# A fused attention and mixture-of-experts kernel: one product step and its loads in other places, and the start of the program issued in other pieces

## The chip, the cores and the metric

The kernel runs on one core of one Trainium2 chip. The metric is the device time of one execution in microseconds (us). The kernel before takes 1173.28 us, the median of three runs that lie between 1173.11 and 1174.34 us.

## The reference

Four batches of N = 5056 tokens have channels C = 256. Attention is taken over channels, so the score matrix of a batch is only 256 x 256, and its result goes token by token to one of eight experts.

```python
# attention over channels, one batch of four: q, k, v are (5056, 256)
qn = q / (norm(q, axis=tokens) + 1e-6)
kn = k / (norm(k, axis=tokens) + 1e-6)
s  = kn.T @ qn / tau                    # (256, 256)
a  = softmax(s, axis=-1)
x  = v @ a                              # (5056, 256)
# experts: x of all batches is (20224, 256), E = 8, F = 1024
logits = x @ w_gate + modality_bias[modality_id]
e = argmax(logits); gate = softmax(logits)[e]
out[token] = gate * (relu(x[token] @ w1[e]) @ w2[e])
```

## The kernel before

**Steps.** A batch is cut into NS = 10 steps of 512 tokens (128 partitions x 4; the last is shorter). `kq_pieces(b, s)` handles step s of batch b: `load` brings q and k (512 KB each) by SP's queue; `split` makes a high and a low half of each on ACT (L320) and DVE (L321), unless the step stands in `WHOLE`, in which case the products are taken from the loaded tile as it is; `mm` adds k'q to the 256 x 256 sum `g` on PE (L365); `square` takes squares on ACT (L344) and adds them on DVE (L346) for the norms. Steps 0 to 5 of batch 1 are whole; its steps 6 to 9 are split. Loaded tiles of batch 1 take turns in two buffers from step 4 on, so step 6 is loaded into the buffer that step 4 had and waits for step 4's squares.

**Routing steps.** After the ten steps and the softmax of batch 0, the program runs through routing steps g = 0 to 39 (10 to a batch). Routing step g takes 512 rows of v, either transposed on PE (L565) or, from g = 6 on, by a transposing DMA into `T` (L534) and four copies `pl` (L511); forms x = v a on PE (`xp`, L585); adds the bias of the modality (L598); counts and places the rows; and scatters them by GpSimd (`xs`, L474) to the region of their expert in DRAM. PLAN says which steps of batch 1 are multiplied in which routing step: here step 5 at g = 6, steps 6 and 7 at g = 8, steps 8 and 9 at g = 9.

**Slots.** From g = 6 on (`first_block`), blocks of 512 rows of one expert, called slots, run beside the routing steps: slot 0 at g = 6, slot 1 at g = 7, and so on. A slot fetches its rows by a transposing DMA (`Tx`, L766) and their gates (`gt`, L769), loads w1 and w2 in two halves each (`w1r`, `w2r`, 512 KB each, L788 and L792), splits them on ACT (L811) and DVE (L818), and runs eight first products `hp_0` to `hp_7` (L845), whose relu goes to `hh` on ACT (L848) and `hl` on DVE (L849), and eight second ones (`y`, L866). Slot 0's rows are of g = 0 to 2. HELD keeps back the scatters of g = 3 and g = 4: they are sent in the following routing step once its rows of tile 3 are copied.

**Order.** The program is written as lists of pieces that `_interleave` mixes by their shares, and each engine then runs its instructions strictly in the order of its own list. SP issues almost all loads; a load whose buffer is still in use or whose source isn't written holds up all that stands behind it. The small loads (`itau`, `wg_sb`, `mb_sb`, the modalities `modraw`) are on SP's queue among the loads of batch 0.

```python
PLAN = [[], [2], [], [3], [4], [], [5], [], [6, 7], [8, 9]]
HELD = {3: 3, 4: 3}
...
if g - 1 in HELD:
    t = HELD[g - 1]
    own.insert(t + 1, lambda: va[g - 1][4]([copied[g, t]]))
```

Of the kernel before, what the change touches and what calls it, by code (L numbers as in the profile page):

```python
# [35 lines left out]
def kernel(  # L36
# [14 lines left out]
    P = 128  # L51
# [28 lines left out]
    PLAN = [[], [2], [], [3], [4], [], [5], [], [6, 7], [8, 9]]  # L80
# [6 lines left out]
    HELD = {3: 3, 4: 3}  # L87
# [87 lines left out]
    turning = []  # L175
    written = [[] for _ in range(G)]
# [14 lines left out]
    def load_small():  # L191
        itau = small["itau"] = const.tile([P, 1], F32, name="itau")
        nc.sync.dma_start(itau, tau.partition_broadcast(P))
        nc.vector.reciprocal(itau, itau)
        wg_sb = small["wg"] = const.tile([P, CH, E], F32, name="wg_sb")
        nc.sync.dma_start(wg_sb, wg.rearrange("(h p) e -> p h e", p=P))
        mb_sb = small["mb"] = const.tile([P, 2, E], F32, name="mb_sb")
        nc.sync.dma_start(
            mb_sb.rearrange("p m e -> p (m e)"), mb.rearrange("m e -> (m e)").partition_broadcast(P)
        )  # L200
# [8 lines left out]
    def load_mod():  # L209

        full = B * (NS - 1)
        raw = p2.tile([P, TT * D], F32, tag="yo", name="modraw").bitcast(I32)
        nc.vector.memset(raw[full // 32 * 32 : R, 2 * PL * TT : 2 * STEP], 0)
        m32 = mod.bitcast(I32).rearrange("(b n) -> b n", b=B)
        for b in range(B):
            nc.sync.dma_start(
                raw[b * (NS - 1) : (b + 1) * (NS - 1), 0 : 2 * STEP],
                m32[b, 0 : 2 * (NS - 1) * STEP].rearrange("(s w) -> s w", w=2 * STEP),
            )
        nc.sync.dma_start(raw[full:R, 0 : 2 * PL * TT], m32[:, 2 * (NS - 1) * STEP : 2 * N])  # L220
        turn["raw"] = raw
# [46 lines left out]
    filled = []  # L268
    acc = {}

    def kq_pieces(b, s, behind=(), later=None):
# [18 lines left out]
        def load():  # L290
            if b == 0:
                begin()
            for n, src, tag in (("q", q, "w1r"), ("k", k, "w2r")):
# [5 lines left out]
                if b == 0 and s == 0:  # L299
                    st[n + "rows"] = rows  # L300
                else:
                    nc.sync.dma_start(st[n][:pp], rows)
            if b == 0 and s == 0:
                for h in range(2):
                    ts = slice(2 * h, 2 * h + 2)
# [23 lines left out]
        def square(h):  # L329
            ts = slice(2 * h, 2 * h + 2)  # L330
            a = acc[b]
            for n, o in (("q", 0), ("k", C)):
# [11 lines left out]
                act(nc.scalar.activation(sq[:pp], st[n][:pp, ts, :], AF.Square))  # L344
                if not first:
                    dve(nc.vector.tensor_tensor(a[:pp, :, o : o + C], a[:pp, :, o : o + C], sq[:pp], ALU.add))  # L346
# [400 lines left out]
    def block_pieces(g, slot, picked, tail):  # L747
# [13 lines left out]
        def load_x():  # L761
# [3 lines left out]
            for ins in (  # L765
# [13 lines left out]
                if slot == 1:  # L779
                    turning.append(ins.ins)  # L780
# [148 lines left out]

    for s in range(NS):  # L930
# [46 lines left out]
    def product(n):  # L977
        g, b, i = tasks[n]
        if n not in products:
            products[n] = list(kq_pieces(  # L980
                b, i, (lambda: routed.get(g, routed[g - 1])) if b == 1 else (),
                squares.setdefault(g + (3 if g + 2 == first_block else 1), [])
# [11 lines left out]
    def products_of(g):  # L994

        out = []
        for n, (at, b, i) in enumerate(tasks):
            if at == g:
                out += [lambda n=n: ask(n)] if g <= first_block else []
                out += product(n)[1:]  # L1000
                if g >= first_block and (b, i) != (1, NS - 1):
                    out.append(lambda n=n: ask(n + (1 if g == first_block else 2)))
        if g == first_block + 1:
            out.append(lambda: ask(min(n for n in range(len(tasks)) if tasks[n][0] > g) + 1))
# [12 lines left out]
    for g in range(G):  # L1017
# [15 lines left out]
        if g - 1 in HELD:  # L1033
            t = HELD[g - 1]
            own.insert(t + 1, lambda: va[g - 1][4]([copied[g, t]]))
        turn = []
# [20 lines left out]
        _interleave(*streams)  # L1057
        if waiting and waiting[0][0] <= g + 1 - lag(g + 1):
            blk = waiting[0][1]
            once(blk, "load")  # L1060
            if blk["slot"] == 0:
                turned(blk["evicted"][-1])
# [94 lines left out]
```

## Time and profile before

| | |
|---|---|
| median of three runs | 1173.28 us |
| profiled execution | 1176.94 us |
| its span, from the first to the last instruction | 1175.1 us |
| mean granted clock of TensorE | 0.998 |
| PE busy | 1152.9 us (98%) |
| DVE busy | 919.4 us (78%) |
| ACT busy | 806.5 us (69%) |

The page gives, for the slowest core, the busy time of each engine, the busy share in slices, the chain that ended last, and the costliest groups of instructions. Times inside the span are counted from its start. A row of the timeline has the start, the duration, the engine, the line of the kernel and the tile that is written and read, and in brackets the idle time just ahead of it with what ended it.

### The profile page before, as it was taken

To read this page: it belongs to the slowest core of one execution; us is meant where nothing else is said; L and a number is where in the kernel's file an instruction comes from. 1 tells how busy PE (TensorE), PEld (TensorE's weight loads), DVE (VectorE), ACT (ScalarE), POOL (GpSimd) and SP (SyncE) were. 2 spreads that over 40 slices of the span, in tenths; PEclk is the share of its full clock that TensorE was granted. 3 is DMA by queue.
4 is the path that set the end of the run, shared out by engine and by line. 5 is a ranking of instruction groups with operands and counts; after the bars stand their busy time and mean duration, and the time that the engine had idled before them with its cause. 6 is when DMAs were issued, how large, how long until landed. Compare 5 with 4: busy or idle time off the path is not lost.

```text
span 1175.1 us, 23436 instructions
## 1 busy us (share of the span) xinstructions
PE 1152.9 (98%) x7748; PEld 1054.9 (90%) x7748; DVE 919.4 (78%) x2590; ACT 806.5 (69%) x1655; POOL 386.9 (33%) x345
## 2 busy tenths in 40 slices
PE   8997999999999999999999999999999999999997
PEld 7886889999999999999999999999999999999997
DVE  6787889898788888888888888878767776685552
ACT  6676877877777777687776777767666666555552
POOL 0054334323333333333333333333333333344122
PEclk9999999999999999999999999999999999999999
DMA  8969999689777677758777766665875665565420
GB/s 311 295 223 235 274 234 261 175 238 218 199 202 198 196 197 207 202 166 228 211 204 209 207 197 165 169 175 162 218 202 174 190 173 156 143 170 144 127 91 30
DMA packets 285843, 228.38 MB, mean 194 GB/s; under 512 B 185064, under 2 KB 243944, under 8 KB 285712
## 3 DMA queue, kind: packets, MB, share of 16 engines
q1 hardware_dynamic: 270032, 185.19, 60.0%
q0 software_dynamic: 15680, 41.61, 10.3%
q8 instruction: 62, 1.02, 0.4%
q14 instruction: 69, 0.57, 0.2%
HBM read 128.79 MB, written 43.43 MB: 147 GB/s over the span
## 4 chain that ended last, share of the span: by engine, by line
PE 84%; issue 7%; DVE 3%; DMA 2%; POOL 2%; ACT 1%; SPq 0%; POOLq 0%; ACTq 0%; DVEq 0%
PE y L866 32%; PE hp L845 32%; PE g L365 10%; PE xp L585 9%; POOL out_dram L474 2%; DMA pl<-T 1%; DMA Tx<-xs 1%; DVE hl L849 0%; DMA xs<-x,pi 0%; DVE inv L398 0%; PE vtp L567 0%; PE gw L434 0%; DVE w2l L818 0%; SPq L511 0%; DMA k<-in_k_dram 0%
## 5 line engine op out<-in xcount | busy, mean ns | idle before, releaser
L866 PE MATMUL y<-w2h,hh 128*128 128x256 f32 x1256 | 354.5, 282 | 0.0
L866 PE MATMUL y<-w2l,hh 128*128 128x256 f32 x1256 | 351.2, 280 | 0.0
L866 PE MATMUL y<-w2h,hl 128*128 128x256 f32 x1256 | 349.5, 278 | 0.1
L474 POOL DMA_INDIRECT xs<-x,pi x160 | 199.1, 1245 | 362.8 <-DVE pr L708 182.8
L474 POOL DMA_INDIRECT out_dram<-yo,gt x158 | 175.2, 1109 | 391.6 <-ACT hh L848 296.8
L845 PE MATMUL hp<-xh,w1h 128*128 128x512 f32 (+1 forms) x640 | 250.0, 391 | 6.1 <-ACT xh L830 3.5
L845 PE MATMUL hp<-xl,w1h 128*128 128x512 f32 (+1 forms) x640 | 250.1, 391 | 0.0
L845 PE MATMUL hp<-xh,w1l 128*128 128x512 f32 (+1 forms) x640 | 248.8, 389 | 0.0
L866 PEld LDWEIGHTS y<-w2h,hh 128*128 128x128 f32 x1256 | 236.4, 188 | 9.5 <-issue 0.2
L866 PEld LDWEIGHTS y<-w2l,hh 128*128 128x128 f32 x1256 | 236.4, 188 | 8.4
L849 DVE SCALAR_TENSOR_TENSOR hl<-hp,hh 128x512 fp32r<-128x512 f32 (+1 forms) x320 | 217.0, 678 | 34.3 <-ACT hh L848 30.8
L866 PEld LDWEIGHTS y<-w2h,hl 128*128 128x128 f32 x1256 | 235.3, 187 | 0.4 <-DVE hl L849 0.3
L848 ACT ACTIVATE hh<-hp 128x512 fp32r<-128x512 f32 (+1 forms) x320 | 188.7, 590 | 59.9 <-PE hp L845 58.7
L811 ACT CAST w1h<-w1r 128x512 fp32r<-128x512 f32 x160 | 99.3, 621 | 169.5 <-PE hp L845 141.2
L818 DVE TENSOR_TENSOR w1l<-w1r,w1h 128x512 fp32r<-128x512 f32 x160 | 110.0, 687 | 90.6 <-ACT w1h L811 87.3
L845 PEld LDWEIGHTS hp<-xh,w1l 128*128 128x128 f32 x640 | 120.1, 188 | 25.8
L845 PEld LDWEIGHTS hp<-xh,w1h 128*128 128x128 f32 x640 | 119.9, 188 | 20.3 <-ACT xh L830 3.7
L845 PEld LDWEIGHTS hp<-xl,w1h 128*128 128x128 f32 x640 | 120.2, 188 | 13.7 <-DVE xl L831 0.4
L818 DVE TENSOR_TENSOR w2l<-w2r,w2h 128x512 fp32r<-128x512 f32 x160 | 109.9, 687 | 12.0 <-ACT w2h L811 9.3
L811 ACT CAST w2h<-w2r 128x512 fp32r<-128x512 f32 x160 | 100.3, 627 | 20.3 <-PE y L866 18.4
L597 DVE COPY x<-xp 128x256 uint16<-128x256 uint16 x136 | 57.1, 420 | 52.3 <-ACT x L596 50.7
L585 PE MATMUL xp<-ah,vh 128*128 128x264 f32 x320 | 92.6, 291 | 1.2 <-DVE L L598 1.2
(162 smaller groups left out, 1827.6 us busy)
## 6 DMA issues: line engine op xcount, KB each, us to landing
w1r<-in_moe_w_dram SPq DMA_DIRECT2D x80, 512.0 KB
w2r<-in_moe_w_dram SPq DMA_DIRECT2D x80, 512.0 KB
q<-in_q_dram SPq DMA_DIRECT2D x35, 512.0 KB
k<-in_k_dram SPq DMA_DIRECT2D x35, 512.0 KB
pl<-T SPq DMA_DIRECT2D x120, 128.0 KB
v<-in_v_dram SPq DMA_DIRECT2D x6, 512.0 KB
xs<-x,pi POOLq DMA_INDIRECT x160
out_dram<-yo,gt POOLq DMA_INDIRECT x158
```

The lines of the kernel that those rows point to most:

```text
L365: nc.tensor.matmul(gram[b][:, m, :], x, y, start=first and m == 0 and i == 0, stop=last and i == len(seq) - 1, skip_group_check=True,)
L474: ins = nc.gpsimd.indirect_dma_start(out=dst, out_offset=bass.IndirectOffsetOnAxis(ap=idx, axis=0), in_=rows, in_offset=None, bounds_check ...
L585: nc.tensor.matmul(xp[:, 0:DE], a[:, h, t * P : (t + 1) * P], w[:, h, :], start=i == 0, stop=i == len(seq) - 1,)
L597: copied[g, t] = nc.vector.tensor_copy(planes[:, 0, :], halfwords[:, 0, :]).ins
L811: ins = nc.scalar.copy(hi, src).ins
L818: evicted[-1] = [ins, nc.vector.tensor_tensor(lo, src, hi.bitcast(F32), ALU.subtract).ins]
L845: nc.tensor.matmul(hp[:, 0:rows], w[:, h, fs], x[:, h, 0:rows], start=i == 0, stop=i == len(seq) - 1)
L848: relu = nc.scalar.activation(hh[:, 0:rows], hp[:, 0:rows], AF.Relu).ins
L849: low = nc.vector.scalar_tensor_tensor(hl[:, 0:rows], hp[:, 0:rows], 0.0, hh[:, 0:rows].bitcast(F32), ALU.max, ALU.subtract).ins
L866: ins = nc.tensor.matmul(y, a[:, tsl], w[:, j % 2, :], start=(j == 0 and i == 0 and t % per == 0), stop=(j == NJ - 1 and i == 2), skip_gro ...
```

## The change

Six things are edited.

1. Twenty products of ones (128 x 128, bf16, nobody reads them) stand ahead of everything else on PE.
2. The q and k of batch 0's step 0 are loaded in three pieces (a quarter, a quarter and a half) instead of two, those of step 1 in two instead of one.
3. The small loads and the modalities are issued by GpSimd instead of SP.
4. PLAN puts step 5 of batch 1 at g = 5, step 6 at g = 7, step 7 at g = 8, and 8 and 9 at g = 9. `products_of` asks for the loads of a routing step ahead of its products; those of step 5 are asked for at g = 4.
5. The scatters of g = 3 no longer wait for copies of g = 4: they are sent first in g = 5, and wait for slot 0's `Tx` and `gt`.
6. The squares of step 3 are taken at the end of g = 5, behind slot 0's first weight splits and ahead of its rows; those of steps 4 and 5 at the end of g = 6. Before, step 5's stood in line with its products.

```diff
-    PLAN = [[], [2], [], [3], [4], [], [5], [], [6, 7], [8, 9]]
+    PLAN = [[], [2], [], [3], [4], [5], [], [6], [7], [8, 9]]
-    HELD = {3: 3, 4: 3}
+    HELD = {3: None, 4: 3}
...
-        nc.sync.dma_start(itau, tau.partition_broadcast(P))
+        nc.gpsimd.dma_start(itau, tau.partition_broadcast(P))
...
-            if b == 0 and s == 0:
-                for h in range(2):
-                    ts = slice(2 * h, 2 * h + 2)
+            if b == 0 and s < 2:
+                for ts in (slice(0, 1), slice(1, 2), slice(2, 4)) if s == 0 else (slice(0, 2), slice(2, 4)):
                     for n in ("q", "k"):
                         nc.sync.dma_start(st[n][:, ts, :], st[n + "rows"][:, ts, :])
...
-                if slot == 1:
-                    turning.append(ins.ins)
+                if slot < 2:
+                    (rows_in, turning)[slot].append(ins.ins)
...
+    warm = ps2.tile([P, 512], F32, tag="aux", bufs=3, name="warm")
+    for i in range(20):
+        nc.tensor.matmul(warm[:, 0:P], onesb, onesb, start=True, stop=True, skip_group_check=True)
+
     for s in range(NS):
         run(kq_pieces(0, s))
...
-                squares.setdefault(g + (3 if g + 2 == first_block else 1), [])
+                squares.setdefault({3: 6, 4: 7, 5: 7}.get(g, g + 1), [])
...
-        for n, (at, b, i) in enumerate(tasks):
-            if at == g:
-                out += [lambda n=n: ask(n)] if g <= first_block else []
-                out += product(n)[1:]
-                if g >= first_block and (b, i) != (1, NS - 1):
-                    out.append(lambda n=n: ask(n + (1 if g == first_block else 2)))
-        if g == first_block + 1:
-            out.append(lambda: ask(min(n for n in range(len(tasks)) if tasks[n][0] > g) + 1))
+        mine = [n for n, task in enumerate(tasks) if task[0] == g]
+        if g <= first_block + 1:
+            out += [lambda n=n: ask(n) for n in mine]
+        if g + 2 == first_block:
+            out += [lambda n=n: ask(n + 1) for n in mine]
+        for n in mine:
+            out += product(n)[1:]
+            if g == first_block + 1:
+                out.append(lambda n=n: ask(n + 1))
+            if g > first_block and tasks[n][1:] != (1, NS - 1):
+                out.append(lambda n=n: ask(n + 2))
...
-        if g - 1 in HELD:
+        if HELD.get(g - 1) is not None:
             t = HELD[g - 1]
             own.insert(t + 1, lambda: va[g - 1][4]([copied[g, t]]))
+        if g + 1 == first_block:
+            own.insert(0, lambda: va[g - 2][4](rows_in))
...
+        if g + 1 == first_block:
+            gap += list(zip(("act", "dve"), waiting[0][1]["evicted"][-1]))
+            run(squares.pop(first_block))
...
             if blk["slot"] == 0:
-                turned(blk["evicted"][-1])
+                turned(newest)
```

**SP's queue, from the transposing load of routing step 8 on, before.** `T_1565` and `T_1611` are the v of routing steps 8 and 9, `q_6` and `k_6` are step 6 of batch 1, the w1r and w2r here are slot 2's weights, and `Tx_1726` is slot 2's rows. What the dots leave out are register instructions.

```order
L534 DMA_TRANSPOSE T_1565<-in_v_dram 128x4x512
L302 DMA q_6_1621<-in_q_dram 128x1024
L302 DMA k_6_1623<-in_k_dram 128x1024
L511 DMA pl_1594<-T_1565 64x2x512 x4
...
L788 DMA w1r_0_1709<-in_moe_w_dram 128x2x512
...
L792 DMA w2r_0_1710<-in_moe_w_dram 128x4x256
L534 DMA_TRANSPOSE T_1611<-in_v_dram 128x4x448
...
L788 DMA w1r_1_1713<-in_moe_w_dram 128x2x512
...
L792 DMA w2r_1_1714<-in_moe_w_dram 128x4x256
...
L766 DMA_TRANSPOSE Tx_1726<-xs 128x4x512
...
L769 DMA gt_1727<-xs 128x4x2
L302 DMA q_7_1888<-in_q_dram 128x1024
```

**The same stretch now.** The numbers behind the names are others: `T_1582` and `T_1624` are the same two loads, `Tx_1747` is slot 2's rows.

```order
L539 DMA_TRANSPOSE T_1582<-in_v_dram 128x4x512
...
L793 DMA w1r_0_1730<-in_moe_w_dram 128x2x512
L516 DMA pl_1607<-T_1582 64x2x512 x4
...
L797 DMA w2r_0_1731<-in_moe_w_dram 128x4x256
...
L793 DMA w1r_1_1734<-in_moe_w_dram 128x2x512
L539 DMA_TRANSPOSE T_1624<-in_v_dram 128x4x448
...
L797 DMA w2r_1_1735<-in_moe_w_dram 128x4x256
...
L771 DMA_TRANSPOSE Tx_1747<-xs 128x4x512
...
L774 DMA gt_1748<-xs 128x4x2
L305 DMA q_6_1784<-in_q_dram 128x1024
L305 DMA k_6_1786<-in_k_dram 128x1024
L305 DMA q_7_2073<-in_q_dram 128x1024
```

`q_6` and `k_6` stood second and third behind the load of routing step 8. They now stand behind the load of routing step 9, slot 2's weights and slot 2's rows; w1r's first half stands ahead of `pl`.

**ACT, slot 1's second and third relu and what stands around them, before.** `hh_2` and `hh_3` are of slot 1, `yo` is slot 0's output, `x_1401` is routing step 7's, `vh_1799` routing step 8's.

```order
L596 COPY x_1401<-xp_1_1786 128x256
L811 CAST w2h_3_1884<-w2r_1_1331 128x512
L571 CAST vh_1799<-vt_0_1803 128x512
L596 COPY x_1401<-xp_2_1818 128x256
L848 ACTIVATE hh_2_1835<-hp_2_1828 128x512
L596 COPY x_1401<-xp_3_1856 128x256
L659 COPY x_1401<-tokid 128x4
L320 CAST qs_6_0_2156<-q_6_1621 128x2x256
L320 CAST ks_6_0_2157<-k_6_1623 128x2x256
L848 ACTIVATE hh_3_1873<-hp_3_1866 128x512
```

**The same place now.** `sq_6_0` are squares of step 6; the other names are those of before with other numbers.

```order
L816 CAST w2h_3_1933<-w2r_1_1368 128x512
L601 COPY x_1434<-xp_2_1855 128x256
L322 CAST qs_6_0_1823<-q_6_1784 128x2x256
L346 ACTIVATE sq_6_0_q<-q_6_1784 128x512
L853 ACTIVATE hh_2_1884<-hp_2_1877 128x512
L322 CAST qs_6_1_1937<-q_6_1784 128x2x256
L322 CAST ks_6_0_1824<-k_6_1786 128x2x256
L346 ACTIVATE sq_6_0_k<-k_6_1786 128x512
L523 COPY vt_0_1840<-pl_1607 128x512
L601 COPY x_1434<-xp_3_1905 128x256
L322 CAST ks_6_1_1938<-k_6_1786 128x2x256
L853 ACTIVATE hh_3_1922<-hp_3_1915 128x512
```

The high halves of q of step 6 (`qs_6_0`) stood behind `hh_2`; they now stand ahead of it, with a square between the two, and those of k stand ahead of `hh_3`.

**PE, the beginning of slot 1's fourth first product, before.** In these names the first number behind `hp`, `xh` and `w1h` is the slot and the second the product.

```order
L845 MATMUL hp_1_3_1866<-xh_1_1553,w1h_1_1_1613 128x512
L845 MATMUL hp_1_3_1866<-xl_1_1554,w1h_1_1_1613 128x512
L845 MATMUL hp_1_3_1866<-xh_1_1553,w1l_1_1_1614 128x512
L845 MATMUL hp_1_3_1866<-xh_1_1553,w1h_1_1_1613 128x512
L845 MATMUL hp_1_3_1866<-xl_1_1554,w1h_1_1_1613 128x512
L845 MATMUL hp_1_3_1866<-xh_1_1553,w1l_1_1_1614 128x512
L866 MATMUL y0_1_1842<-w2h_1_0_1487,hh_1_1_1770 128x256
```

**The same place now.**

```order
L590 MATMUL xp_7_3_1905<-ah_0_463,vl_7_1433 128x264
L850 MATMUL hp_1_3_1915<-xh_1_1570,w1h_1_1_1626 128x512
L850 MATMUL hp_1_3_1915<-xl_1_1571,w1h_1_1_1626 128x512
L370 MATMUL g_1_510<-qs_1_6_0_1823,ks_1_6_0_1824 128x256 x2
L850 MATMUL hp_1_3_1915<-xh_1_1570,w1l_1_1_1627 128x512
L850 MATMUL hp_1_3_1915<-xh_1_1570,w1h_1_1_1626 128x512
L850 MATMUL hp_1_3_1915<-xl_1_1571,w1h_1_1_1626 128x512
L850 MATMUL hp_1_3_1915<-xh_1_1570,w1l_1_1_1627 128x512
L370 MATMUL g_1_510<-qs_1_6_0_1823,ks_1_6_0_1824 128x256 x10
L871 MATMUL y0_1_1891<-w2h_1_0_1510,hh_1_1_1795 128x256
```

The first twelve products of step 6 (`g_1`, from `qs_1_6_0` and `ks_1_6_0`) now stand inside `hp_1_3`, behind its first two matmuls. Before, they stood within slot 2.

## Rows read from the trace of the kernel before

**Rows 1.** From the page: the busy time of each engine, and the chain that ended last by engine.

```profile
PE 1152.9 (98%) x7748; PEld 1054.9 (90%) x7748; DVE 919.4 (78%) x2590; ACT 806.5 (69%) x1655; POOL 386.9 (33%) x345
...
PE 84%; issue 7%; DVE 3%; DMA 2%; POOL 2%; ACT 1%; SPq 0%; POOLq 0%; ACTq 0%; DVEq 0%
```

**Rows 2.** What PE waited for between 80 and 160 us: engine, tile and line that waits, what ended the wait, us in total, times, longest.

```profile
PE hp L845 <- ACT xh L830: 3.5, 1, 3.5
PE hp L845 <- DVE hl L849: 2.6, 3, 1.7
PE g L365 <- DVE qs L321: 1.6, 2, 1.1
PE xp L585 <- DVE L L598: 1.2, 1, 1.2
PE g L365 <- DVE ks L321: 0.2, 1, 0.2
```

**Rows 3.** Stretches of the span as PE saw them: the stretch and its length, busy time of PE with its matmuls, the granted clock, the share of the DMA engines, GB/s.

```profile
0.00:5.00 5.00, 0.37 (x1) 1.00 0.55 172
5.00:10.00 5.00, 5.00 (x13) 1.00 0.95 358
10.00:15.00 5.00, 5.00 (x25) 1.00 1.03 419
...
94.00:97.00 3.00, 0.11 (x1) 1.00 0.96 286
97.00:100.00 3.00, 3.00 (x15) 1.00 1.36 235
...
150.00:160.00 10.00, 8.02 (x55) 1.00 1.11 191
...
170.00:500.00 330.00, 329.99 (x2280) 1.00 0.77 208
...
1168.00:1172.00 4.00, 0.00 (x0) 0.78 0.26 81
```

**Rows 4.** Timeline of PE, its first row.

```profile
4.63 13.55 PE L365 MATMUL g<-q,k 128*128 128x256 f32 x50 [4.63 <-DMA k<-in_k_dram]
```

**Rows 5.** Timeline of SP's queue from 84 to 145 us. The duration of a row is the time for which the issue held up the queue.

```profile
88.14 2.46 SPq L766 DMA_TRANSPOSE Tx<-xs  x1
...
92.53 6.09 SPq L534 DMA_TRANSPOSE T<-in_v_dram  x1
...
106.80 3.30 SPq L766 DMA_TRANSPOSE Tx<-xs  x1
...
110.98 0.39 SPq L788 DMA_DIRECT2D w1r<-in_moe_w_dram  x1
...
112.11 6.78 SPq L534 DMA_TRANSPOSE T<-in_v_dram  x1
118.99 0.52 SPq L302 DMA_DIRECT2D q<-in_q_dram  x1
119.57 0.42 SPq L302 DMA_DIRECT2D k<-in_k_dram  x1
...
124.34 0.41 SPq L788 DMA_DIRECT2D w1r<-in_moe_w_dram  x1
...
126.60 2.34 SPq L534 DMA_TRANSPOSE T<-in_v_dram  x1
...
131.54 6.27 SPq L766 DMA_TRANSPOSE Tx<-xs  x1
...
138.49 0.49 SPq L302 DMA_DIRECT2D q<-in_q_dram  x1
```

**Rows 6.** Timeline of ACT, the rows that waited for a DMA or stand at step 6.

```profile
94.50 1.38 ACT L518 COPY xt<-Tx 128x512 uint16<-128x512 uint16 x2 [3.93 <-DMA Tx<-xs]
...
116.25 0.62 ACT L811 CAST w1h<-w1r 128x512 fp32r<-128x512 f32 x1 [2.19 <-DMA w1r<-in_moe_w_dram]
...
126.61 1.42 ACT L518 COPY vt<-pl 128x512 uint16<-128x512 uint16 x2 [0.50 <-DMA pl<-T]
128.31 0.62 ACT L811 CAST w1h<-w1r 128x512 fp32r<-128x512 f32 x1 [0.27 <-DMA w1r<-in_moe_w_dram]
...
133.88 0.62 ACT L320 CAST qs<-q 128x512 fp32r<-128x512 f32 x1
```

**Rows 7.** Timeline of PE: slot 1's fourth first product, and the products of step 6.

```profile
133.32 0.39 PE L845 MATMUL hp<-xh,w1h 128*128 128x512 f32 x1
133.55 0.40 PE L845 MATMUL hp<-xl,w1h 128*128 128x512 f32 x1
133.79 0.39 PE L845 MATMUL hp<-xh,w1l 128*128 128x512 f32 x1
...
154.90 0.28 PE L365 MATMUL g<-qs,ks 128*128 128x256 f32 x1
156.25 0.38 PE L365 MATMUL g<-qs,ks 128*128 128x256 f32 x1 [1.08 <-DVE qs L321]
156.85 1.45 PE L365 MATMUL g<-qs,ks 128*128 128x256 f32 x10 [0.22 <-DVE ks L321]
...
159.66 0.38 PE L365 MATMUL g<-qs,ks 128*128 128x256 f32 x1 [0.52 <-DVE qs L321]
```

More of the change, by code (lines that the diff above doesn't have):

```diff
@@ L175 @@
     turning = []
+    rows_in = []
     written = [[] for _ in range(G)]
@@ L192, in load_small @@
         itau = small["itau"] = const.tile([P, 1], F32, name="itau")
-        nc.sync.dma_start(itau, tau.partition_broadcast(P))
+        nc.gpsimd.dma_start(itau, tau.partition_broadcast(P))
         nc.vector.reciprocal(itau, itau)
         wg_sb = small["wg"] = const.tile([P, CH, E], F32, name="wg_sb")
-        nc.sync.dma_start(wg_sb, wg.rearrange("(h p) e -> p h e", p=P))
+        nc.gpsimd.dma_start(wg_sb, wg.rearrange("(h p) e -> p h e", p=P))
         mb_sb = small["mb"] = const.tile([P, 2, E], F32, name="mb_sb")
-        nc.sync.dma_start(
+        nc.gpsimd.dma_start(
             mb_sb.rearrange("p m e -> p (m e)"), mb.rearrange("m e -> (m e)").partition_broadcast(P)
@@ L215, in load_mod @@
         for b in range(B):
-            nc.sync.dma_start(
+            nc.gpsimd.dma_start(
                 raw[b * (NS - 1) : (b + 1) * (NS - 1), 0 : 2 * STEP],
@@ L219, in load_mod @@
             )
-        nc.sync.dma_start(raw[full:R, 0 : 2 * PL * TT], m32[:, 2 * (NS - 1) * STEP : 2 * N])
+        nc.gpsimd.dma_start(raw[full:R, 0 : 2 * PL * TT], m32[:, 2 * (NS - 1) * STEP : 2 * N])
         turn["raw"] = raw
@@ L268 @@
     filled = []
+    newest = []
+    gap = []
     acc = {}
@@ L302, in load @@
                     nc.sync.dma_start(st[n][:pp], rows)
-            if b == 0 and s == 0:
-                for h in range(2):
-                    ts = slice(2 * h, 2 * h + 2)
+            if b == 0 and s < 2:
+                for ts in (slice(0, 1), slice(1, 2), slice(2, 4)) if s == 0 else (slice(0, 2), slice(2, 4)):
                     for n in ("q", "k"):
@@ L343, in square @@
                         sq = p3.tile([P, 2, C], F32, tag="vt", name=f"sq_{b}_{s}_{h}_{n}")
-                act(nc.scalar.activation(sq[:pp], st[n][:pp, ts, :], AF.Square))
+                squared = nc.scalar.activation(sq[:pp], st[n][:pp, ts, :], AF.Square)
+                act(squared)
                 if not first:
-                    dve(nc.vector.tensor_tensor(a[:pp, :, o : o + C], a[:pp, :, o : o + C], sq[:pp], ALU.add))
+                    added = nc.vector.tensor_tensor(a[:pp, :, o : o + C], a[:pp, :, o : o + C], sq[:pp], ALU.add)
+                    dve(added)
+                    newest[:] = [squared.ins, added.ins]
         def mm(h):
@@ L980, in product @@
             products[n] = list(kq_pieces(
-                b, i, (lambda: routed.get(g, routed[g - 1])) if b == 1 else (),
-                squares.setdefault(g + (3 if g + 2 == first_block else 1), [])
+                b, i, (lambda: gap if g + 3 == first_block else routed.get(g, routed[g - 1])) if b == 1 else (),
+                squares.setdefault({3: 6, 4: 7, 5: 7}.get(g, g + 1), [])
                 if b == 1 and (g < first_block or i == NS - 1) else None,
```

## Prediction

> **What bounds the kernel now.** I read the page's busy times and chain first, then what PE waited for, then PE's stretches, and last the queues of SP, ACT and PE around the places that the diff moves. PE is busy for 98% of the span and holds 84% of the chain [rows 1]: PE's matmuls set the time, and only what PE loses can be won. The stretches show where it loses [rows 3]: the first 5 us hold one matmul, the next 5 us 13 where the 5 us after that hold 25, so the first dozen run at half rate (1.2 and then 2.4 GHz); some us go between 80 and 160, among them 2.9 us between 94 and 97 and 2.0 us between 150 and 160; from 170 to 500 us PE loses 0.01 of 330 us. So whatever PE has gained or lost by 170 us is carried to the end, since from there the order of its work is that of before. The waits between 80 and 160 us add up to some 9 us [rows 2]: 3.5 for slot 0's rows (`xh`), 2.6 for `hl`, 1.8 for the halves of steps 6 and 7 (`qs`, `ks`), 1.2 for the biased logits `L`.
>
> **The start.** PE's first product waits 4.63 us for k [rows 4]. The pieces of a quarter bring this forward, and the twenty products of ones let the clock rise while PE waits. The half rate costs (25 - 13) x 0.2 = 2.4 us. But the loads bound this: three steps are 3.15 MB, and the first 10 us move 0.86 + 1.79 = 2.65 MB; at 419 GB/s the third step's last byte comes at 11.2 us at the earliest [rows 3]. Before, the first two steps (32 matmuls in the trace, two to a product) end at 10 + (32 - 14) x 0.2 = 13.6 us, so at most 13.6 - 11.2 = 2.4 us are gained by then, and at least nothing; I take 1.0, nearer to the low end since the DMA engines are already at a share of 0.95 and the same bytes go through them. The small loads by GpSimd share those engines; I cost them at nothing, covered by the loads of steps 5 to 9, which come well ahead of PE. If that cover failed, PE would wait within the first 43 us and the 1.0 would go.
>
> **Around slot 0.** The squares of step 3 leave ACT and DVE ahead of the logits on which PE waits 1.2 us, and the scatters of g = 3 leave GpSimd while `Tx` is on its way: `Tx` is issued at 88.14 and its first reader starts at 94.50, 6.4 us later [rows 5, 6], where PE waits 3.5 us. The square of step 5 leaves the stretch in which `hl` is late. Bounds are 0 and 3.5 + 1.2 + 2.6 = 7.3 us, of which the weight splits and `pl`, which stay, hold the most; I take 1.7, the longest wait for `hl`, about a quarter.
>
> **Step 6 of batch 1, the term that decides.** Before, its loads are issued at 118.99 and 119.57, right behind the load of routing step 8 [rows 5]; ACT has its first half at 133.88 [rows 6], and PE multiplies it only from 154.90 on [rows 7], so some 30 us lie between issue and use. The change takes this slack from both sides. The loads now stand behind the load of routing step 9, all of slot 2's weights and slot 2's `Tx` and `gt`; the use comes ahead of `hh_2` on ACT and behind two matmuls of slot 1's `hp_3` on PE, which is where PE stands at 133.79 [rows 7].
>
> When are they issued? Three times a transposing load is followed within some 5 us by a second one, and the second holds up SP's queue: the end of its issue lies 92.53 + 6.09 - 88.14 = 10.5, 112.11 + 6.78 - 106.80 = 12.1 and 131.54 + 6.27 - 126.60 = 11.2 us behind the issue of the first, where one that has no other just ahead takes 2.34 to 3.30 [rows 5]. The load of routing step 9 can't go before `pl` has emptied its tile: it was issued at 126.60, when the last `pl` landed (its reader starts at 126.61) [rows 5, 6]. With the 1 MB of step 6 no longer ahead, and slot 0 a little earlier, I put it between 124.6 and 126.6 and take 125.2. Then slot 2's `Tx` has left the queue at 125.2 + 11.2 = 136.4; `gt` and q go by 136.9, k 0.6 later at 137.5, as before [rows 5]. A load of 512 KB takes 128.31 - 124.34 = 4.0 to 116.25 - 110.98 = 5.3 us from issue to its reader here [rows 5, 6]; I take 4.7, so k is there at 142.2, and with one copy of 0.62 by ACT [rows 6] the first product can run at 142.8. The ends are 124.6 + 10.5 + 0.5 + 0.6 + 4.0 + 0.6 = 140.8 and 126.6 + 12.1 + 0.5 + 0.6 + 5.3 + 0.6 = 145.7. PE, which has matmuls strictly in order, stands until then, and so do ACT and DVE, whose next instructions are the splits of step 6 with slot 1's `hh_2` and `hl_2` behind them.
>
> Against before that is 142.8 - 133.8 = **+9.0 us** (7.0 to 11.9) at the same point of PE's work. Since this end is set by SP's queue, the gains of the start and of slot 0 don't come off it: PE merely waits longer. What does come off are the 2.0 us that PE loses between 150 and 160 [rows 3], where steps 6 and 7 both had to be split, 1.08 + 0.22 + 0.52 of it by their halves [rows 7]; with one of the two gone from there I take all 2.0, and 1.0, half of it, for the low end.
>
> **The clock after such a wait.** PE would idle for some 9 to 11 us. After the last matmul of before the mean granted clock of 1168 to 1172 us is 0.78, so it falls within 5 us; but after the 3.5 us of idle time up to 96.89 the stretch from 97 on has a clock of 1.00 [rows 3]. A fall would cost between nothing and the 2.4 us of the start; I take 1.2, since the splits of step 6 space the first products after the wait in any case.
> The Trainium skill, "TensorE: Matmul & The Clock Gate" (section "HAM oscillation — how this bites in real kernels"), says that a wait for loads of this kind lets the clock drop, so that the work behind it starts cold each time. By that rule the sum would take the whole 2.4 us and end at 1182.7; by the row from 97 us on alone it would take nothing and end at 1180.3. No row of before has a wait this long in the middle of the program.
>
> **The sum.** 9.0 - 2.0 + 1.2 = +8.2 us on the profiled execution (1176.94 to 1185.1); taken over to the median of the runs, 1173.28 + 8.2 = **1181.5 us**. Its own range is 1173.3 + 7.0 - 2.0 + 0 = 1178.3 to 1173.3 + 11.9 - 1.0 + 2.4 = 1186.6.
>
> **Rivals.**
> Step 6 is there in time, and the kernel is faster. For this k must have landed by about 131, so its issue must lie by 126, ahead of the load of routing step 9; the order speaks against it, since `Tx` stands between, and for it only that the whole queue of SP might run several us earlier once `Tx` of slot 0 is earlier. From an issue at 126 on this rival loses. Then the gains all count: 1.0 + 1.7 + 2.0 = 4.7, or 1168.6 us.
> `Tx` of slot 2 holds up the queue no longer than a lone one. Then it leaves at 124.6 + 2.34 + 0.7 + 3.3 = 130.9, k is issued at 132.0, is there at 136.0 and multiplied at 136.6: +2.8 - 2.0 = +0.8, or 1174.1 us, no change that can be told. Three of three pairs speak against it.
> The wait costs more than the sum has: step 7's and step 8's loads also stand behind step 6's on SP, and the backlog of ACT and DVE after the wait makes PE wait again for `hl`; this is the upper end above.
> That the change doesn't do what it says is no case here: the start's gain may be nothing, but in the likeliest case it falls into the wait and isn't seen in the time.
>
> **Chances.** The wait for step 6: 0.72. In time: 0.17. The short hold-up: 0.11. A measurement of this kernel tells differences over 0.2% (2.35 us) from no change. The first case's own range lies above 1175.6, so slower 0.72, same 0.11, faster 0.17. The range of 8 in 10 takes in the first case but for a little at its end and the second rival, and reaches toward the first rival, leaving out most of it: 1170.5 to 1186.7.
>
> **What the profile after should show.** PE's first product at about 3 to 4 us with 0.2 us between products from then on, or from 6 us; slot 0's `hp_0` ahead of 96.9; on SP a `Tx` of some 6 us ahead of q and k of step 6, issued near 137; on ACT `qs_6_0` waiting for a DMA for several us; on PE one wait of 8 to 12 us inside slot 1's `hp_3`, and no waits for `qs` and `ks` around 155. The forecast is wrong if q of step 6 is issued before 130, or if PE's wait there stays under 3 us.

## The result, and the profile after

The change makes the kernel slower. Five runs of each: 1183.11 us (1182.52 to 1184.03) against 1174.34 (1173.11 to 1177.27), a ratio of 1.0073 with an interval from 1.0057 to 1.0089, or +8.8 us (6.7 to 10.5). In a second job the ratio was 1.0070 (1.0051 to 1.0088). The forecast was 1181.5 us. The profiled execution took 1182.66 us with a span of 1180.8; the one of before took 1176.94 with 1175.1, so the two traces differ by 5.7 us, and these are what the rows below explain.

From the page, the busy time of the engines, as in [rows 1]:

```profile
PE 1157.3 (98%) x7768; PEld 1058.3 (90%) x7768; DVE 920.6 (78%) x2590; ACT 807.2 (68%) x1655; POOL 386.0 (33%) x353
```

PE still holds the chain (88% of it). Its own busy time has grown by 4.4 us. The twenty products of ones hold 2.3 us of that (1.20 to 3.51 us); the rest are matmuls that ran slower, since no other work was added on PE. What PE waited for between 0 and 170 us, the longer ones (engine, tile and line, what ended the wait, us, times, longest):

```profile
PE g L370 <- ACT ks L322: 7.6, 1, 7.6
PE rp L646 <- DVE oh L621: 3.0, 1, 3.0
...
PE hp L850 <- DVE hl L854: 0.9, 1, 0.9
```

One wait stands out: the products of step 6 (`g`) wait 7.6 us for `ks`. The waits of [rows 2] for `xh`, `L`, `qs` and for most of `hl` are gone; a wait of 3.0 us for `oh` is new. PE's stretches, columns as in [rows 3]:

```profile
0.00:5.00 5.00, 3.63 (x23) 1.00 0.52 150
5.00:10.00 5.00, 4.84 (x16) 1.00 0.95 303
...
130.00:140.00 10.00, 2.95 (x22) 0.85 1.11 275
140.00:145.00 5.00, 4.45 (x21) 0.61 0.79 283
145.00:150.00 5.00, 5.00 (x40) 1.00 0.78 247
150.00:160.00 10.00, 10.00 (x66) 1.00 1.25 238
...
170.00:500.00 330.00, 329.99 (x2279) 1.00 0.77 207
```

From 130 to 140 us PE is busy for 2.95 of 10. After that the granted clock is 0.61 and the 5 us hold 21 matmuls where the next 5 hold 40. From 150 to 160 PE loses nothing, where it lost 2.0 us [rows 3], and from 170 to 500 us nothing again: at slot 3's first matmul, here before and now, the new kernel is 5.3 us late, and this is carried to the end of the span.

```profile
181.57 0.39 PE L845 MATMUL hp<-xh,w1h 128*128 128x512 f32 x1
```

```profile
186.91 0.39 PE L850 MATMUL hp<-xh,w1h 128*128 128x512 f32 x1
```

The queue that made the wait, SP's, from 84 to 150 us (the duration is the time for which the issue held up the queue, as in [rows 5]):

```profile
88.75 2.03 SPq L771 DMA_TRANSPOSE Tx<-xs  x1
...
92.77 4.55 SPq L539 DMA_TRANSPOSE T<-in_v_dram  x1
...
106.21 2.78 SPq L771 DMA_TRANSPOSE Tx<-xs  x1
...
110.99 4.96 SPq L539 DMA_TRANSPOSE T<-in_v_dram  x1
...
124.01 1.55 SPq L539 DMA_TRANSPOSE T<-in_v_dram  x1
...
127.09 4.73 SPq L771 DMA_TRANSPOSE Tx<-xs  x1
...
132.57 0.43 SPq L305 DMA_DIRECT2D q<-in_q_dram  x1
133.05 0.42 SPq L305 DMA_DIRECT2D k<-in_k_dram  x1
```

q of step 6 was issued at 118.99 [rows 5]; it now goes at 132.57, behind slot 2's `Tx`, which itself came right behind the load of routing step 9 and held the queue up for 4.73 us. Then ACT (as in [rows 6]) and PE (as in [rows 7]) at the place of use:

```profile
137.84 0.62 ACT L322 CAST qs<-q 128x512 fp32r<-128x512 f32 x1 [7.91 <-DMA q<-in_q_dram]
138.37 0.63 ACT L346 ACTIVATE sq_q<-q 128x512 f32<-128x512 f32 x1
138.90 0.58 ACT L853 ACTIVATE hh<-hp 128x512 fp32r<-128x512 f32 x1
139.37 0.61 ACT L322 CAST qs<-q 128x512 fp32r<-128x512 f32 x1
139.88 0.61 ACT L322 CAST ks<-k 128x512 fp32r<-128x512 f32 x1
```

ACT stands for 7.91 us until q has landed, 5.3 us after its issue. Then come a split, a square and `hh_2`, another split, and only as the fifth instruction the `ks` on which PE waits.

```profile
132.32 0.40 PE L850 MATMUL hp<-xh,w1h 128*128 128x512 f32 x1
132.56 0.40 PE L850 MATMUL hp<-xl,w1h 128*128 128x512 f32 x1
140.55 0.80 PE L370 MATMUL g<-qs,ks 128*128 128x256 f32 x2 [7.60 <-ACT ks L322]
141.15 0.63 PE L850 MATMUL hp<-xh,w1l 128*128 128x512 f32 x1
141.57 0.63 PE L850 MATMUL hp<-xh,w1h 128*128 128x512 f32 x1
...
142.85 1.82 PE L370 MATMUL g<-qs,ks 128*128 128x256 f32 x10
144.51 0.28 PE L871 MATMUL y<-w2h,hh 128*128 128x256 f32 x1
```

PE did two matmuls of slot 1's `hp_3` at 132.32 and 132.56, stood for 7.60 us, and from 141.15 on spaced its matmuls by 0.42 us instead of 0.24 [rows 7].

### The profile page after: what moved, and what is told of

Its sections match the earlier page's. It is cut to its first block, busy times and chain, and to the rows that moved or that the text cites. A ratio compares the mean times of both kernels' runs of the same rounds, so it can differ in the third digit from the quotient of the medians.

```text
span 1180.8 us, 23492 instructions
## 1 busy us (share of the span) xinstructions
PE 1157.3 (98%) x7768; PEld 1058.3 (90%) x7768; DVE 920.6 (78%) x2590; ACT 807.2 (68%) x1655; POOL 386.0 (33%) x353
## 4 chain that ended last, share of the span: by engine, by line
PE 88%; issue 5%; DMA 2%; POOL 2%; DVE 1%; ACT 1%; SPq 0%; POOLq 0%; DVEq 0%; ACTq 0%
PE y L871 34%; PE hp L850 34%; PE xp L590 10%; PE g L370 10%; POOL out_dram L479 2%; DMA w2r<-in_moe_w_dram 1%; DMA k<-in_k_dram 1%; DMA q<-in_q_dram 0%; PE vtp L572 0%; SPq L309 0%; PE gw L439 0%; DVE vl L577 0%; PE atp L433 0%; DVE w1l L823 0%; DVE w2l L823 0%
## 5 line engine op out<-in xcount | busy, mean ns | idle before, releaser
L479 POOL DMA_INDIRECT xs<-x,pi x160 | 196.0, 1225 | 359.4 <-DVE pr L713 184.0
L479 POOL DMA_INDIRECT out_dram<-yo,gt x158 | 172.5, 1092 | 399.6 <-ACT hh L853 301.9
```

Source lines behind the costliest of these rows:

```text
L479: ins = nc.gpsimd.indirect_dma_start(out=dst, out_offset=bass.IndirectOffsetOnAxis(ap=idx, axis=0), in_=rows, in_offset=None, bounds_check ...
```

## The experiments

Two theories were set against each other. Q (queue): the loss is the distance between the landing of step 6's loads, which SP's queue sets, and PE's arrival at the place of use, and nothing else counts much. P (place): step 6's products within slot 1 cost by themselves, whatever the loads do, since their splits go ahead of `hh_2` and `hl_2` on ACT and DVE. Smaller rivals were the start, the scatters and the clock. The expectations were given on the scale of 1173.3 us for the kernel before; since that kernel ran at 1175.4 to 1176.9 beside these runs, each table row gives the ratio to it with its interval, and that ratio x 1173.28. The expectations of e1, e3 and e4 count from the change's 1183.1 us, which is 1181.8 on this scale.

| run | what | ratio | x 1173.28 |
|---|---|---|---|
| after | the change | 1.0073 (1.0057 to 1.0089) | 1181.8 |
| e1_early_load | loads early | 1.0044 (1.0030 to 1.0057) | 1178.4 |
| e2_late_use | loads late, use late | 1.0016 (1.0006 to 1.0027) | 1175.2 |
| e3_fill | PE kept busy ahead of step 6 | 1.0081 (1.0068 to 1.0094) | 1182.8 |
| e4_no_start | after without the start | 1.0066 (1.0051 to 1.0082) | 1181.0 |
| e6_after_again | the change, second job | 1.0070 (1.0051 to 1.0088) | 1181.5 |
| e7_early_load_held | e1 and scatters as before | 1.0048 (1.0032 to 1.0064) | 1178.9 |
| e8_start_only | before with the start | 1.0007 (0.9995 to 1.0018) | 1174.1 |
| e9_step6_alone | before, use in g = 7 | 1.0037 (1.0021 to 1.0053) | 1177.6 |
| e10_step6_start | e9 and the start | 1.0026 (1.0015 to 1.0037) | 1176.3 |
| e11_held | after, scatters as before | 1.0073 (1.0057 to 1.0090) | 1181.8 |

**e1_early_load.** The loads of step 6 are asked for at the end of g = 6, ahead of the load of routing step 9; the use stays in g = 7.

```diff
+        if g == first_block:
+            out += [lambda n=n: ask(n) for n, task in enumerate(tasks) if task[0] == g + 1]
```

> The changed kernel, with step 6 of batch 1 asked for one routing step earlier, so that its two loads stand ahead of the load of routing step 9 and of slot 2's rows on SP; its products and splits stay in routing step 7. Theory Q (the wait comes from the place of the two loads in SP's queue): q is issued at 122 to 124 instead of 132.6, PE's wait of 7.6 us within slot 1's hp_3 falls below 1.5 us, the clock stays at its full level there, and some of the time that PE saved between 150 and 160 comes back: 1183.1 - 7.6 - 2.4 + 0 to 3 = 1173 to 1176 us. Rival P (the place of the products is the cause: splits of step 6 ahead of hh_2 hold ACT and DVE and so PE, whenever the loads come): PE still loses over 4 us there, 1179 us or more.

SP's queue, PE's stretches and PE's waits of this kernel:

```profile
125.99 0.35 SPq L305 DMA_DIRECT2D q<-in_q_dram  x1
```

```profile
100.00:110.00 10.00, 7.41 (x28) 0.68 1.03 289
...
130.00:140.00 10.00, 10.00 (x74) 1.00 1.11 258
```

```profile
PE rp L646 <- DVE oh L621: 5.5, 1, 5.5
PE hp L850 <- DVE xl L836: 2.4, 1, 2.4
```

q is issued 6.6 us earlier than in the changed kernel (122 to 124 was expected), the wait in `hp_3` is gone, and PE is busy for 10 of 10 us from 130 to 140. The time fell by only 0.3% against the change, not by the 0.6 to 0.9% expected. In this execution PE had lost time earlier, 5.5 us for the counts (`rp` on `oh`) and 2.4 us for `xl`, and from 100 to 110 us its clock was 0.68. So the wait was made by the late load, but its removal was worth about 3 us of 8. Theory P's loss at the place of use doesn't show either: from 130 to 150 us PE has no wait in this trace.

**e2_late_use.** The loads stay behind `Tx`; the products of step 6 go back to g = 8, where they stood before.

```diff
-    PLAN = [[], [2], [], [3], [4], [5], [], [6], [7], [8, 9]]
+    PLAN = [[], [2], [], [3], [4], [5], [], [], [6, 7], [8, 9]]
+        if g == first_block + 1:
+            out += [lambda n=n: ask(n) for n, task in enumerate(tasks) if task[1:] in ((1, 6), (1, 7))]
```

> The changed kernel, with the products of steps 6 and 7 back in routing step 8, as before the change; the loads of step 6 keep their late place behind slot 2's rows on SP. Theory Q with its second half (the wait is the distance between the load's landing at about 138 and its first use): the loads land at about 138 as in the changed kernel, the use is again at about 154, so no wait for them; the losses between 150 and 160 of before (about 3 us) are back: 1173 to 1175 us. Rival (the late loads cost time wherever they are used, by what they push behind them on SP): 1178 us or more.

PE's stretch around `hp_3` in this kernel:

```profile
130.00:140.00 10.00, 10.00 (x72) 1.00 1.02 308
```

q is issued at 132.54, as late as in the change, and PE is busy for 10 of 10 us there and again from 150 to 160. All but 0.16% of the loss is gone: 1.0016 against 1.0073, about 6.7 us. The time, 1175.2, is just above the expectation's upper end of 1175. With Q alone e1 and e2 should have come out alike; e2 is better by 0.28%, and this speaks for P. It is not shown by rows: what PE loses in e1's trace behind slot 0 stands at 160.26 us (1.02 for `hl`) and from 165.24 on (1.07 and 0.22 at the next step's products), not where step 6 is used.

**e3_fill.** 115 products of ones, which nobody reads, between the first two matmuls of `hp_3` and the rest, with all twelve products of step 6 behind them, to keep PE busy over the wait and so the clock up.

```diff
+                if slot == 1 and j == 3 and i < 2:
+                    for _ in range(115 if i else 0):
+                        fill = nc.tensor.matmul(
+                            busy[:, 0:P], onesb, onesb, start=True, stop=True, skip_group_check=True
+                        )
```

> The changed kernel, with 115 products of ones that nobody reads on PE just ahead of the first product of step 6, behind the first two matmuls of slot 1's hp_3, so that PE works through most of its wait of 7.6 us. Theory C (the clock falls in the wait, and the half rate behind it costs): the wait ends at the same 140.5 us, matmuls behind it are at full rate, and 2.4 us come back: 1180.7 us (1180 to 1181.5). Rival (behind the wait PE is held by the splits on ACT and DVE in any case, so the rate doesn't matter): 1183 us, as the changed kernel.

The time doesn't tell what it was meant to: PE came to `hp_3` only at 139.37 us in this execution, so the fill ran until 146.24 and was itself the delay, while q had landed at 140.18. But the rows behind the fill show the price of the clock:

```profile
146.24 1.67 PE L371 MATMUL g<-qs,ks 128*128 128x256 f32 x12
...
148.67 0.28 PE L887 MATMUL y<-w2h,hh 128*128 128x256 f32 x1
```

The twelve products and the four matmuls of `hp_3` take 2.43 us here, at a granted clock of 1.00 from 140 to 150 us; in the change the same sixteen take 3.96 (140.55 to 144.51). The difference is 1.5 us.

**e4_no_start.** The changed kernel without the products of ones, with the pieces and the small loads as before.

```diff
-            if b == 0 and s < 2:
-                for ts in (slice(0, 1), slice(1, 2), slice(2, 4)) if s == 0 else (slice(0, 2), slice(2, 4)):
+            if b == 0 and s == 0:
+                for ts in (slice(0, 2), slice(2, 4)):
...
-    warm = ps2.tile([P, 512], F32, tag="aux", bufs=3, name="warm")
-    for i in range(20):
-        nc.tensor.matmul(warm[:, 0:P], onesb, onesb, start=True, stop=True, skip_group_check=True)
```

> The changed kernel without its new start: no products of ones, loads of batch 0's steps 0 and 1 in the pieces of before, small loads on SP again. Theory Q (the end of the wait is set by SP's queue, which PE's lead doesn't move): PE is later by about 1 us up to the wait, the wait is shorter by as much, and the time is that of the changed kernel, 1182.5 to 1184 us. Rival (what the start gains is carried to the end): 1184 us or more, by 1 us or more above the changed kernel in the same job.

The same time as the change. PE's wait in `hp_3` in this trace, then the same row in the second pair's trace of the change (e6_after_again) and in e11_held:

```profile
145.69 0.80 PE L370 MATMUL g<-qs,ks 128*128 128x256 f32 x2 [1.86 <-ACT ks L322]
```

```profile
142.41 0.80 PE L370 MATMUL g<-qs,ks 128*128 128x256 f32 x2 [8.25 <-ACT ks L322]
```

```profile
142.78 0.79 PE L370 MATMUL g<-qs,ks 128*128 128x256 f32 x2 [7.29 <-ACT ks L322]
```

In e4 PE came to `hp_3` 10.9 us later than in the change, at 143.19, and its wait is 1.86 us; where it came at 133.5 it waited 8.25. Only about 1 us of the 10.9 was expected from the start; the rest is other waits of this execution (2.57 us for k at 38.26, 5.5 for the counts ahead of slot 0). The product starts between 140.55 and 145.69 in all four, though PE's arrival spans 10.9 us (132.3, 133.5, 134.6 and 143.2). So about half of what happens earlier is swallowed by the wait in these traces; it is not all, since q itself was issued later in e4, at 137.35, behind the same `Tx`.

**e5_before_again** and **e6_after_again.** The two kernels once more, in a second job.

> The kernel before, unchanged, for a profile from the chip of these runs. If the waits around slot 0 (rows of routing step 5 and first products, 80 to 105 us) come from the change, PE loses about 5 us there, as in the first profile; if they are the chip's, it loses 8 us or more here too.

> The changed kernel, unchanged, beside the others on one chip. Theory Q: one wait for step 6 inside slot 1's hp_3, of 2 to 8 us, the shorter the later PE comes there; time 1.005 to 1.009 of the kernel before. If the waits ahead of slot 0's first products vary from chip to chip, PE is at slot 1's hp_3 between -1 and +10 us against before, and the wait makes up for the difference.

The kernel before took 1175.09 us with a span of 1173.3 and the changed one had a span of 1183.6: +10.3 us, where the first pair has +5.7. PE's wait for `ks` is there again, 8.25 us, and the clock stays down longer (0.50 from 140 to 145 us, 0.67 from 145 to 150). So the wait and the clock repeat, and their sizes vary by some us from execution to execution. Ahead of slot 0 PE waited 4.9 us in e5 (0.20 and 4.69, the latter for `xh`) and 3.6 in e6, so the waits there are no larger with the change in this pair.

**e7_early_load_held** and **e11_held.** The scatters of g = 3 wait again as before, once with the early loads of e1 and once in the changed kernel.

```diff
-    HELD = {3: None, 4: 3}
+    HELD = {3: 3, 4: 3}
...
-        if g + 1 == first_block:
-            own.insert(0, lambda: va[g - 2][4](rows_in))
```

> The early load of step 6 (as in e1_early_load), and the scatters of routing step 3 sent again as before, behind the copies of routing step 4. In the changed kernel they were issued at 82.8, before slot 0's weights had landed, and not behind slot 0's rows. Theory S (these scatters delay slot 0's weights, and PE waits for what stands behind the splits): PE's wait for the counts of routing step 5 (rp), 5.5 us in e1_early_load, falls under 2 us, slot 0's hp_0 comes by 97, and the time falls by 3 to 5 us against e1_early_load, to about that of before (ratio 0.998 to 1.001). Rival W (the weights' splits stand ahead of routing step 5's counts on DVE, whenever the scatters go): the wait stays over 4 us and the ratio stays at 1.003 or more.

> The changed kernel with the scatters of routing step 3 sent again as before, behind the copies of routing step 4; all else as changed, the late load of step 6 too. Theory S: slot 0's weights land earlier without them, PE's wait for the counts of routing step 5 (2.9 to 5.8 us in the runs of the change) falls under 2 us; but the wait for step 6 then grows by as much, and the time stays: ratio 1.006 to 1.009. Rival: the wait for the counts stays at 2.9 us or more, since the splits stand ahead of the counts on DVE.

Neither moves the time against its partner (1.0048 and 1.0044; 1.0073 and 1.0073): the scatters' place costs nothing that can be told. PE's wait for `oh` fell to 1.9 and 1.7 us, under 2 as theory S has it, but the time did not fall with it, and PE waits another 1.8 and 1.9 us for `run` of the same counts, so the wait for the counts is there with the scatters held too. What is left of the loss when the load is early shows in e7, on PE's timeline, in its stretch, and on ACT's timeline:

```profile
132.55 0.38 PE L370 MATMUL g<-qs,ks 128*128 128x256 f32 x1 [1.83 <-ACT ks L322]
133.37 3.10 PE L370 MATMUL g<-qs,ks 128*128 128x256 f32 x11 [0.44 <-DVE qs L323]
```

```profile
130.00:140.00 10.00, 7.71 (x31) 0.66 1.21 241
```

```profile
129.84 0.62 ACT L322 CAST qs<-q 128x512 fp32r<-128x512 f32 x1 [1.65 <-DMA q<-in_q_dram]
```

PE waits 1.83 us for `ks` of step 6 and 0.44 us for `qs` at its new place, and the granted clock of the stretch is 0.66, after waits much shorter than the one of the change. The first of them is for the most part the load once more: q was issued at 123.82, ACT stood for 1.65 us until it could split it at 129.84, and `ks` (131.90) is the fifth of ACT's instructions from there. Only the 0.44 us is left for theory P.

**e8_start_only, e9_step6_alone, e10_step6_start.** The kernel before with only the start; with only step 6 at g = 7 and its loads where they were; with both.

```diff
-    PLAN = [[], [2], [], [3], [4], [], [5], [], [6, 7], [8, 9]]
+    PLAN = [[], [2], [], [3], [4], [], [5], [6], [7], [8, 9]]
...
+                out += [lambda n=n: ask(n + 1)] if g == first_block + 2 else []
...
-                    out.append(lambda n=n: ask(n + (1 if g == first_block else 2)))
-        if g == first_block + 1:
-            out.append(lambda: ask(min(n for n in range(len(tasks)) if tasks[n][0] > g) + 1))
+                    out.append(lambda n=n: ask(n + (1 if g <= first_block + 1 else 2)))
```

> The kernel before with only the new start: products of ones, loads of steps 0 and 1 in smaller pieces, small loads by GpSimd. The prediction's term: 1.0 us gained by 43 us and carried to the end, ratio 0.9991 (0 to 2.4 us, 0.998 to 1.000). Rival: the smaller pieces only move the wait to the third step's loads, and the products of ones don't keep the clock up: ratio 1.000 or more.

> The kernel before with one part of the change alone: step 6 of batch 1 multiplied in routing step 7 and step 7 in 8, step 5 staying in routing step 6, and all else as before; its loads keep the place of before, issued near 119, ahead of the load of routing step 9. Theory Q: they land by 125, some 5 us ahead of their first use, so no wait over 1 us for them, and part of the 2.0 us lost between 150 and 160 is saved: ratio 0.9975 to 1.000. Rival P (splits of step 6 beside slot 1's relus hold PE wherever the loads stand): PE loses 2 us or more around slot 1's hp_2 and hp_3, ratio 1.001 or more.

> The same with the new start of the change (products of ones, smaller pieces, small loads by GpSimd). By the run of the start alone (ratio 1.0007) it changes nothing: the same ratio as e9_step6_alone within 0.001. If the start's 1.4 us, which are there at slot 0's first product, are carried to the end here, the ratio is lower by 0.001.

The start alone is no change that can be told (1.0007): in its trace slot 0's `hp_0` is 1.4 us earlier than before, slot 1's `hp_3` 1.8 us later (135.10), and slot 3's first matmul 0.14 us earlier (181.43). Step 6 in g = 7 with an early load costs 0.26 to 0.37% without the rest of the change; in the time, that is rival P and not theory Q, which had 0.9975 to 1.000. e9's kernel was run once more for a trace.

**e12_step6_alone_again.**

> The kernel of e9_step6_alone for a profile, since the profiled execution of that run was disturbed. Its ratio of 1.0037 speaks for a loss of some 4 us against before although the loads come early. If the loss lies at the products of step 6 (rival P), PE's waits for qs, ks or hl between 125 and 150 us add up to 3 us or more beyond those of before; if it lies ahead of slot 0's first products, as in e1_early_load, these lose 3 us there and little behind.

ACT's row and PE's rows of it:

```profile
142.94 0.62 ACT L320 CAST qs<-q 128x512 fp32r<-128x512 f32 x1 [4.27 <-DMA q<-in_q_dram]
```

```profile
132.46 0.39 PE L365 MATMUL g<-qs,ks 128*128 128x256 f32 x1 [1.46 <-DVE qs L321]
...
145.35 0.50 PE L845 MATMUL hp<-xh,w1h 128*128 128x512 f32 x1 [2.09 <-DVE hl L849]
```

PE waits 1.46 us for a half of step 6 at its new place; ACT made its own halves just ahead without waiting for a load, so this is price of the place, theory P. And the mechanism of the change is back one step later: ACT waits 4.27 us for q of step 7, which was issued at 138.77 behind slot 2's `Tx`; `hh` stands behind that split, so PE waits 2.09 us for `hl`. The two waits add up to 3.55 us, the 3 us or more of rival P, but the larger one is theory Q's. The run, a single one, took 1179.0 us beside 1176.01.

## Why the prediction was right, point by point

**The step that decides** came out as forecast: `q` and `k` behind slot 2's `Tx`, one wait of PE behind the first two matmuls of `hp_3`, with ACT standing beside it. Undoing it from either side (e1, e2) ends that wait, and e4 and e11 show that it absorbs much of what comes ahead. Its size in the first pair was +6.8 us (140.55 against 133.79) where 9.0 was forecast, with 7.0 as the low end; in the second pair it was +9.9 (142.41 against e5's 132.56). Three terms in it were mis-sized. The pair of transposing loads held SP for less: from the issue of the first to the end of the second 8.6, 9.7 and 7.8 us (127.09 + 4.73 - 124.01), not 10.5 to 12.1 (the last of the three decides, and 11.2 was taken for it), and the load of routing step 9 went at 124.01 instead of 125.2, so q left at 132.57, 4.3 us ahead of the forecast. Landing took 5.3 us, not 4.7. And between the landing and PE's product lay not one copy of 0.6 us but five instructions of ACT, 2.7 us (137.84 to 140.55). The first of these errors made the forecast too late and the other two too early, so they partly cancel.

**The clock.** It fell, to 0.61 for the stretch from 140 to 145. From the first product at 140.55 to the next product of another kind at 144.51 PE did twelve products of step 6 and four matmuls of `hp_3` in 3.96 us; at the full clock, 0.117 and 0.235 us apart, they take 2.34. The difference is 1.6 us (1.5 against e3's rows), against 1.2 taken and 0 to 2.4 as bounds. The row of 3.5 us of idle time with a clock of 1.00 behind it [rows 3] was no safe guide: the same kernel's second execution (e5) waited 4.69 us at that place, and the granted clock was 0.72 from 90 to 100 us. The Trainium skill, "TensorE: Matmul & The Clock Gate" (section "HAM oscillation — how this bites in real kernels"), says that work behind such a wait for loads starts cold; this trace agrees, with 0.61 from 140 to 145 us.

**150 to 160 us.** The 2.0 us that PE lost there are gone, as forecast (10.00 of 10). By the starts of matmuls the new kernel makes good 3.0 us between 144.51 and slot 3; the other 1.0 is no idle time in either trace and stays unexplained. The trace's sum is then 6.8 + 1.6 - 3.0 = +5.4, beside the span's +5.7, where 9.0 + 1.2 - 2.0 = +8.2 was forecast. That the medians differ by +8.8, near the forecast, is in part luck: the profiled execution of before was 2.6 us above its median, that of the change 0.5 below. The second pair, +10.3, shows that single executions scatter around it.

**The start.** The first product came at 3.68 us instead of 4.63, but at the end of batch 0's products PE was 0.57 us ahead (its norms at 41.76 against 42.33), not the 1.0 taken. The products of ones did not end the half rate: matmuls came at half rate until some 7.5 us, and the stretch from 5 to 10 us holds 16 of them, not 25. (The clock column says 1.00 for these stretches in both kernels, so the rate is read from the counts.) At `hp_3` PE was 1.0 us ahead (132.32 against 133.32), where the start's 1.0 and slot 0's 1.7 were forecast. As forecast the gain fell into the wait (e4), and without that wait it is too small to tell (e8).

**Slot 0** is the step that failed. 1.7 us of gain were forecast, and `hp_0` came 0.96 us later, at 97.85 (some 0.9 us of that is order: seven more products of `xp` and one more set of counts now stand ahead of it). The waits for `L` and `xh` went, but a new one of 3.0 us came ahead of them: PE waits for `oh` at 88.81, and `oh` stands on DVE behind the low half of slot 0's w1, which stands behind ACT's high half:

```profile
86.35 1.14 ACT L816 CAST w1h<-w1r 128x512 fp32r<-128x512 f32 x2 [2.82 <-DMA w1r<-in_moe_w_dram]
```

ACT waited 2.82 us for the w1r load. But PE's and DVE's rows of the same counts, before and then now, show that `oh` did not come late:

```profile
87.47 3.19 PE L365 MATMUL g<-q,k 128*128 128x256 f32 x14
90.49 0.18 PE L641 MATMUL rp<-oh,trim 128*128 128x32 bf16 x1
```

```profile
89.90 0.21 DVE L616 TENSOR_TENSOR oh<-val,vm 128x32 bf16<-128x32 f32 x1
```

```profile
81.68 3.62 PE L370 MATMUL g<-q,k 128*128 128x256 f32 x16
...
88.81 0.19 PE L646 MATMUL rp<-oh,trim 128*128 128x32 bf16 x1 [3.04 <-DVE oh L621]
```

```profile
88.52 0.23 DVE L621 TENSOR_TENSOR oh<-val,vm 128x32 bf16<-128x32 f32 x1
```

`oh` was made at 88.52 us, 1.4 us earlier than before. What is missing is work: before, fourteen whole products of batch 1 ran on PE from 87.47 until the counts; with step 5 at g = 5 a whole set of sixteen runs from 81.68, and PE stands until `oh` is made. Behind the wait the granted clock fell, to 0.86 from 90 to 100 us. The sum asked which waits would go and not what the moved products had covered. No run moves step 5 back alone, so this is read from rows and not tested. Also wrong was the reading that the scatters of g = 3 would wait for slot 0's `Tx`. GpSimd's timeline:

```profile
82.80 1.21 POOL L479 DMA_INDIRECT xs<-x,pi  x1 [0.30 <-ACT vh L576]
```

They went from 82.80 us on, before `Tx` was issued at 88.75 [after's SP rows], and waited for nothing of slot 0; item 5 of the change says otherwise and is wrong there.

**The rivals.** "In time" did not come: q was issued at 132.57, behind the limit of 126. The short hold-up came nearer than its chance of 0.11 says. Three second transposing loads were again longer (4.55 to 4.96) than lone ones (1.55 to 2.78), but from the issue of routing step 9's load to the end of slot 2's `Tx` it was 7.8 us, and 6.8 to 7.3 in e2, e3, e4, e6 and e11; that rival's sum has 6.3, the forecast 11.2. Its time did not come because the landing and ACT's five instructions took longer than it had. That the backlog of ACT and DVE behind the wait costs more was not seen: `hl` has 0.9 us in all, at 109.00, ahead of the wait.

**The signs.** Seen were the first product at 3 to 4 us, ACT's wait for q, and no wait for `qs` and `ks` around 155. Missed were `hp_0` ahead of 96.9 (97.85), a `Tx` of some 6 us (4.73), q near 137 (132.57) and a wait of 8 to 12 us (7.6). Neither sign of being wrong came: q was not issued before 130, and the wait was not under 3 us.

**What is left open.** With the load early, 0.26 to 0.48% remain (e1, e7, e9, e10). Named by rows are late loads once more (step 6's in e7, step 7's behind `Tx` in e12, where ACT waits 4.27 us, and in e10, 4.14), the low halves of step 6 at the new place (1.46 us in e12, 0.53 in e10, 0.44 in e7), and clock falls behind short waits. For e1 and e7 slot 0 may come on top: in the eight traces of kernels with step 5 at g = 5, `hp_0` came at 97.2 to 106.7 us, after 100 in six of them, and at 95.5 to 98.4 in the five traces without it (the kernel before twice, e8, e10, e12). In the change itself the wait for step 6 hides most of this. How much each part costs, and why e2, whose `hp_0` came at 102.68, still lost only 0.16%, the runs don't settle. No version tried beats the kernel before.

## What to carry to other kernels

When work is moved earlier, move its loads by the queue and not by the plan: find what stands ahead of them on the issuing queue, add the landing time and every instruction between landing and use, and compare with the time at which the bound engine arrives. A wait of that kind swallows gains made ahead of it, so gains at the start are tested without it. Ask also what the moved work covered where it stood: the bound engine may now wait there. And with the loads early 0.26 to 0.48% was still lost, of which rows show only a part as the price of the early use itself.

## What the runs showed of the hardware that was not expected

- The granted clock fell after much shorter waits than the one of the change: 0.66 from 130 to 140 us in e7, behind waits of 1.83 and 0.44 us in that stretch, and 0.68 from 100 to 110 us in e1, which has a wait of 2.4 us for `xl` in that stretch. In the kernel before, 3.5 us of idle time were followed by 1.00 [rows 3], and 4.69 us at the same place in e5 by 0.50.
- Twenty products of ones from 1.2 to 3.5 us did not bring the first real products to the full rate: that came at some 7.5 us.
- A second transposing load held SP's queue up for 4.55 to 4.96 us here, and 6.09 to 6.78 in the kernel before [rows 5], at the same places. It is no fixed price: slot 2's `Tx` took 2.99 us in e2 and 3.98 in e6, behind the same load.
- PE's wait for the counts ahead of slot 0 was 3.0 and 2.9 us in two executions of the changed kernel and 5.5 in e1, whose edit issues its first load only at 125.99.
